# Retention scores masked on three engines, and a weight conversion without its sign step, started at another pace

## The chip, the cores and the metric

The kernel runs on one core of a Trainium2 chip. The metric is the device time of one execution in microseconds (us), and less is better. Five engines work side by side, each through its own instruction stream in order, and wait for one another by semaphores: TensorE does the matrix products, VectorE, ScalarE and GpSimd the element-wise work, and SyncE issues the transfers (DMAs). In the profile they are PE (PEld for its weight loads), DVE, ACT, POOL and SP.

## The reference, cut to what matters

```python
# 4 batches x 8 heads, 576 tokens, head size 64
scores = (1 / sqrt(64)) * q @ k.T
gamma  = 1 - 2.0 ** (-5 - head)
ret    = scores * where(i >= j, gamma ** (i - j), 0)
x  = (ret @ v), heads joined           # 2304 tokens x 512
h  = x @ w_in                          # 512 -> 2048
x2 = (h * clip(h + 3, 0, 6) / 6) @ w_out     # 2048 -> 512
h2 = x2 @ w2_in                        # 512 -> 1024
solu = h2 * softmax(h2)
out  = layernorm(solu) * g_ln @ w2_out # 1024 -> 512
```

All weights arrive as 64-bit floats, read as pairs of 32-bit integers: index 1 is the upper word (sign, 11 bits of exponent, 20 of mantissa), index 0 the lower.

## The kernel before, in words

**Products in two parts.** Each large product takes every operand as a coarse part plus a rest (both float32r) and adds three products of 128 x 128 weights with 512 columns. So each activation and each weight is split: ScalarE copies the value to the coarse part, and GpSimd or VectorE subtracts to get the rest.

**Attention.** It runs over 16 pairs of heads (`pr` 0 to 15). For each pair TensorE makes `s` (scores of four diagonal blocks of 128 keys by 128 queries for two heads, 128 x 1024 in PSUM, one buffer), `u` (states of four chunks), `z` (the last 64 tokens), and for the pair before it `xp` (values from masked scores and from states, one buffer). VectorE turns `s` into `st` with one multiplication by a mask (L334) that holds one constant for each head, and zeros where the key comes later than the query. ScalarE scales the values `v` by a decay for each key (L320), VectorE steps the states (L350) and multiplies the result by a decay for each query from `tab_sb` (L387, `xa`), and ScalarE and GpSimd split that into `xb`, the input of the next layer.

**Weight conversion.** `Weights.split` (from L112) turns a block of 128 x 512 doubles into coarse part and rest. ScalarE scales the upper words as floats into `wz` (L119). VectorE shifts left by 3 (L122), puts the sign back (L123), masks the exponent out (L124), scales the lower word by it (L125) and adds (L128). ScalarE copies the sum to the coarse part (L130), and VectorE, for every third block GpSimd, subtracts for the rest (L132). Raw data are loaded ahead into two `wraw` buffers, each free again after L125 has read it. There are 48 conversions in the run: 12 during attention (six blocks for `w_in`, then six for `w_out`), 20 more for the other `w_in` and `w_out` blocks from about 190 to 350 us, and 16 for the last layer.

**Order.** Attention yields three times for each pair, so a step `s` counts three to a pair. A conversion is issued at steps 5, 6, 8, 9, 11, 12 and so on (two of three, from pair 1) until the 12 are out. From pair 5 on, two pieces of the next layer (`mlp_a`, six matmuls each) go into every step. A scheduler then sets each engine's order from this; it is fixed when the program is built.

Of the kernel before, what the change touches and what calls it, by code (L numbers as in the profile page):

```python
# [9 lines left out]
F32 = mybir.dt.float32  # L10
# [13 lines left out]
NFF2 = DFF2 // 128  # L24
FA = 6
GAMMA = [1.0 - 2.0 ** (-5 - h) for h in range(H)]
N_DEC = 128 * (H // 2) + H + H // 2
NPAIR = NH // 2
NV = 5
BLOCKS = [(0, 512), (512, 512), (1024, 512), (1536, 512), (2048, 256)]  # L30
# [3 lines left out]
C_ORDER = (2, 4, 3, 0, 1)  # L34
NX = 10
STEP_B = 12
W_LOAD = 4
W_FROM = 5
A_FROM = 5
TAIL = 2  # L40
ACT_W = (1,)
# [14 lines left out]


@with_exitstack
def retention_hardswish_solu_kernel(ctx, tc, kt, qt, kn, vt, w1, w2i, w2o, gln, decay, out):


    nc = tc.nc
    ve, se, ge = nc.vector, nc.scalar, nc.gpsimd
# [25 lines left out]
    class Weights:  # L89
# [22 lines left out]
        def split(self, raw, w, scale=None, done=None):  # L112


            z = p0.tile([128, 512], F32, tag="wz", bufs=2, name="wz")
            t = p0.tile([128, 512], I32, tag="wt", bufs=2, name="wt")
            zi, f = z.bitcast(I32), t.bitcast(F32)

            first = se.activation(out=z, in_=raw[:, :, 1].bitcast(F32), func=ACTF.Copy, scale=2.0 ** -112)  # L119
            if self.pin:  # L120
                tc.keep_in_program_order(first)
            ve.tensor_scalar(out=t, in0=zi, scalar1=3, scalar2=None, op0=ALU.logical_shift_left)  # L122
            ve.scalar_tensor_tensor(out=t, in0=zi, scalar=-2 ** 31, in1=t, op0=ALU.bitwise_and, op1=ALU.bitwise_or)  # L123
            ve.tensor_scalar(out=zi, in0=t, scalar1=-2 ** 23, scalar2=None, op0=ALU.bitwise_and)  # L124
            ve.scalar_tensor_tensor(  # L125
                out=z, in0=raw[:, :, 0].bitcast(U32), scalar=2.0 ** -52, in1=z, op0=ALU.mult, op1=ALU.mult
            )
            ve.tensor_tensor(out=f, in0=f, in1=z, op=ALU.add)  # L128
            if scale is None:
                se.activation(out=w[:, 0], in_=f, func=ACTF.Copy)  # L130
                eng = ge if self.at % 3 == 2 else ve
                eng.tensor_tensor(out=w[:, 1], in0=f, in1=f32(w[:, 0]), op=ALU.subtract)  # L132
            else:
                se.activation(out=w[:, 0], in_=f, func=ACTF.Copy, scale=scale)
                ve.scalar_tensor_tensor(
                    out=w[:, 1], in0=f, scalar=scale, in1=f32(w[:, 0]), op0=ALU.mult, op1=ALU.subtract
                )
            if done:
                done()
# [130 lines left out]
    pa = tc.alloc_tile_pool(name="pa", bufs=1)  # L270
    ps_a = tc.alloc_tile_pool(name="ps_a", bufs=1, space=bass.MemoryType.PSUM)

    decay_sb = pa.tile([128, N_DEC], F32, name="decay_sb")
    tab_sb = [pa.tile([128, S], F32, name=f"tab_sb{p}") for p in range(NP)]
    mask = pa.tile([128, NP, 2, 128], F32, name="mask")
    mask4 = pa.tile([128, NP, 64], F32, name="mask4")
    raws, vs, sts, sts4, states, us, xps = {}, {}, {}, {}, {}, {}, {}
    HEADS = [slice(0, 64), slice(64, 128)]
    CHUNKS = [slice(128 * c, min(128 * c + 128, S)) for c in range(NV)]
# [5 lines left out]
    def mm_a(*args, **kw):  # L285
        tc.keep_in_program_order(nc.tensor.matmul(*args, **kw))  # L286

    def load_pair(pr):

        if pr >= NPAIR:  # L290
            return
        early = pr < EARLY
        if early:
            raw = p0.tile([128, 3, S], F32, tag="w", bufs=FA, name=f"raw{pr}")
            rk, rq, rn = raw[:, 0], raw[:, 1], raw[:, 2, :512]
        else:
            rk = pa.tile([128, S], F32, tag="rk", bufs=2, name=f"rk{pr}")
            rq = pa.tile([128, S], F32, tag="rq", bufs=3, name=f"rq{pr}")
            rn = pa.tile([128, 512], F32, tag="rn", bufs=2, name=f"rn{pr}")
        nc.sync.dma_start(out=rk, in_=kt[pr])  # L300
        nc.sync.dma_start(out=rq, in_=qt[pr])
        if pr == 0:
            nc.sync.dma_start(out=decay_sb, in_=decay)
        if early:
            rv = p0.tile([128, 2 * NV, D], F32, tag="g", bufs=FA, name=f"rv{pr}")
        else:
            rv = pa.tile([128, 2 * NV, D], F32, tag="rv", bufs=2, name=f"rv{pr}")
        nc.sync.dma_start(out=rv, in_=vt[pr])
        nc.sync.dma_start(out=rn, in_=kn[pr])
        raws[pr] = rk, rq, rn.rearrange("p (c d) -> p c d", d=128), rv  # L310

    def prep(pr):

        if pr >= NPAIR:
            return
        rv = raws[pr][3]
        v = vs[pr] = pa.tile([128, 2, NV, D], F32, tag="v", bufs=2, name=f"v{pr}")
        for h in range(2):
            head = 128 * NP + 2 * (pr % NP) + h
            se.activation(  # L320
                out=v[:, h].rearrange("p c d -> p (c d)"),
                in_=rv[:, NV * h:NV * h + NV].rearrange("p c d -> p (c d)"),
                func=ACTF.Copy, scale=decay_sb[:, head:head + 1],
            )

    def scores(pr):

        st = sts[pr] = pa.tile([128, 2, 512], F32, tag="st", bufs=2, name=f"st{pr}")
        sp = ps_a.tile([128, 2, 512], F32, tag="s", bufs=1, name=f"s{pr}")
        k, q, _, _ = raws[pr]  # L330
        for c in range(4):
            for h in range(2):
                mm_a(sp[:, h, CHUNKS[c]], k[HEADS[h], CHUNKS[c]], q[HEADS[h], CHUNKS[c]], start=(c == 0), stop=(c == 3))
        ve.tensor_tensor(  # L334
            out=st.rearrange("p h (c q) -> p h c q", q=128), in0=sp.rearrange("p h (c q) -> p h c q", q=128),
            in1=mask[:, pr % NP].unsqueeze(2).to_broadcast([128, 2, 4, 128]), op=ALU.mult,
        )

    def chunk_states(pr):

        rn, v = raws[pr][2], vs[pr]
        up = ps_a.tile([128, 4, 64], F32, tag="u", bufs=1, name=f"u{pr}")
        state = states[pr] = pa.tile([128, 4, 64], F32, tag="state", bufs=2, name=f"state{pr}")
        for c in range(4):
            for h in range(2):
                mm_a(up[HEADS[h], c], rn[:, c, HEADS[h]], v[:, h, c], start=(c == 0), stop=(c == 3))
        at = 128 * NP + H + pr % NP
        se.activation(out=state[:, 0], in_=up[:, 0], func=ACTF.Copy)
        for c in range(1, 4):
# [94 lines left out]
    g_a = lambda ff: (p0, "g", FA)
    mlp_a = chain.from_iterable(mlp(t, list(range(FA)), g_a, evac_partial) for t in range(3))
# [189 lines left out]
    first = {}  # L635
# [19 lines left out]
    t = B_ORDER[-1]  # L655
# [63 lines left out]
```

## Time and profile before

| what | value |
|---|---|
| median of 3 runs | 715.96 us (714.98 to 716.06) |
| the profiled execution, its own time | 715.41 us |
| its span, first to last instruction | 713.7 us |
| TensorE busy | 680.6 us, 95% of the span |
| VectorE, ScalarE, GpSimd busy | 441.9, 307.2, 249.1 us |
| TensorE busy 0 to 90 us, and 90 to 200 us | 67.63 of 90, 110.00 of 110 us |
| TensorE busy 200 to 360, and 360 to 520 us | 152.36 of 160, 160.00 of 160 us |
| mean granted clock of TensorE | 0.978 |

The profiled execution's time is its span and 1.71 us around it. A stretch in which TensorE is busy from end to end is not proof that TensorE is at its best there, but one with gaps shows that something else came last. The attention pairs can be followed by the scores matmuls, which open each pair.

### The profile page before, as it was taken

The numbers are of one execution on the slowest core, as the hardware profiler recorded it, in microseconds if no ns is written. First come the engines' busy times: TensorE is split into PE (matmuls) and PEld (weight loads), VectorE is DVE, ScalarE is ACT, GpSimd is POOL, SyncE is SP. The second block draws the span as 40 slices with busy tenths as digits, with TensorE's granted clock in tenths as the row PEclk, the third lists the DMA queues.
The fourth block names the chain that finished last, engine by engine and source line by source line (L and its number), as shares of the span: only waits on it lengthen the run. The fifth ranks groups of instructions, "written<-read, shape, count | busy, mean of one in ns | idle before, by whom it ended". The sixth has DMA issues, their size and how long they took to land.

```text
span 713.7 us, 10518 instructions
## 1 busy us (share of the span) xinstructions
PE 680.6 (95%) x3968; PEld 560.5 (79%) x3968; DVE 441.9 (62%) x673; ACT 307.2 (43%) x536; POOL 249.1 (35%) x233
## 2 busy tenths in 40 slices
PE   7577899999998999999999999999999999999998
PEld 5565677788886997778778888889988888888887
DVE  3899943240496387925777785411178877776780
ACT  4335442342544435433524524413247555454453
POOL 2233341240533133353633502422236633331333
PEclk8789999999999999999999999999999999999999
DMA  9676666113151533315568365013655643233233
GB/s 332 230 227 206 202 191 197 58 45 74 59 192 45 178 110 100 116 56 181 179 198 272 125 228 180 29 45 130 251 166 133 148 89 74 69 80 74 60 82 81
DMA packets 76259, 97.96 MB, mean 137 GB/s; under 512 B 42672, under 2 KB 44976, under 8 KB 75184
## 3 DMA queue, kind: packets, MB, share of 16 engines
q1 hardware_dynamic: 76208, 97.29, 45.1%
q8 instruction: 31, 0.51, 0.3%
q14 instruction: 20, 0.16, 0.1%
HBM read 63.71 MB, written 24.12 MB: 123 GB/s over the span
## 4 chain that ended last, share of the span: by engine, by line
PE 70%; DVE 12%; DMA 7%; issue 5%; ACT 3%; POOL 1%; SPq 0%; DVEq 0%; POOLq 0%; ACTq 0%
PE h L189 17%; PE x L210 16%; PE o L625 14%; PE h L559 14%; DMA wraw<-in_w_dram 6%; PE acc L210 4%; PE xp L286 3%; DVE wt L122 2%; DVE wt L123 2%; DVE wz L125 2%; ACT wz L119 1%; DVE wt L128 1%; PE s L286 1%; DVE wz L124 1%; PE u L286 1%
## 5 line engine op out<-in xcount | busy, mean ns | idle before, releaser
L204 POOL TENSOR_TENSOR g<-gf,g 128x512 fp32r<-128x512 f32 (+1 forms) x80 | 101.4, 1269 | 218.4 <-ACT g L203 194.7
L210 PE MATMUL x<-g,w 128*128 128x512 f32 x648 | 154.6, 393 | 3.0 <-DVE gf L200 1.5
L210 PEld LDWEIGHTS x<-g,w 128*128 128x128 f32 x648 | 120.0, 188 | 31.1 <-DVE gf L200 2.2
L189 PE MATMUL h<-xb,w 128*128 128x512 f32 (+1 forms) x600 | 137.3, 366 | 3.9 <-ACT w L130 2.4
L189 PEld LDWEIGHTS h<-xb,w 128*128 128x128 f32 x600 | 101.8, 193 | 22.4 <-ACT w L130 2.8
L200 DVE SCALAR_TENSOR_TENSOR gf<-r,h 128x512 f32<-128x512 f32 (+1 forms) x80 | 50.3, 629 | 87.2 <-ACT r L199 70.0
L559 PE MATMUL h<-w2i,x2b 128*128 128x512 f32 x432 | 102.0, 389 | 0.0
L625 PE MATMUL o<-w2o,lt 128*128 128x512 f32 (+1 forms) x456 | 101.0, 378 | 0.0
L625 PEld LDWEIGHTS o<-w2o,lt 128*128 128x128 f32 x456 | 82.5, 188 | 16.0
L559 PEld LDWEIGHTS h<-w2i,x2b 128*128 128x128 f32 x432 | 80.6, 188 | 16.3
L189 PE MATMUL h<-xB,w 128*128 128x512 f32 x360 | 82.4, 389 | 0.0
L180 POOL TENSOR_TENSOR lt<-lT,lt 128x512 fp32r<-128x512 f32 x36 | 46.3, 1305 | 93.8 <-ACT lt L179 93.8
L189 PEld LDWEIGHTS h<-xB,w 128*128 128x128 f32 x360 | 67.6, 188 | 14.0
L203 ACT ACTIVATE g<-gf 128x512 fp32r<-128x512 f32 (+1 forms) x80 | 46.9, 587 | 64.3 <-DVE gf L200 64.2
L199 ACT ACTIVATE r<-h,half 128x512 f32<-128x512 f32 (+1 forms) x80 | 50.7, 636 | 40.1 <-PE h L189 39.8
L210 PE MATMUL acc<-g,w 128*128 128x256 f32 (+1 forms) x312 | 63.8, 328 | 0.7 <-ACT x2p L262 0.5
L122 DVE TENSOR_SCALAR wt<-wz 128x512 int32<-128x512 int32 x48 | 33.4, 695 | 39.4 <-ACT wz L119 39.0
L210 PEld LDWEIGHTS acc<-g,w 128*128 128x128 f32 x312 | 50.5, 191 | 8.3 <-POOL g L204 1.0
L180 POOL TENSOR_TENSOR xb<-xa,xb 128x512 fp32r<-128x512 f32 (+7 forms) x32 | 29.1, 927 | 59.9 <-ACT xb L179 59.9
L128 DVE TENSOR_TENSOR wt<-wt,wz 128x512 f32<-128x512 f32 x48 | 44.8, 934 | 0.6
L119 ACT ACTIVATE wz<-wraw 128x512 f32<-128x512 f32 x48 | 31.5, 662 | 26.7 <-DMA wraw<-in_w_dram 21.4
L130 ACT ACTIVATE w<-wt 128x512 fp32r<-128x512 f32 x32 | 20.2, 631 | 45.0 <-DVE wt L128 45.0
(77 smaller groups left out, 744.1 us busy)
## 6 DMA issues: line engine op xcount, KB each, us to landing
wraw<-in_w_dram SPq DMA_DIRECT2D x32, 512.0 KB, 4.2
rv<-in_vt_dram SPq DMA_DIRECT2D x16, 320.0 KB, 4.7
x2l<-x2s SPq DMA_DIRECT2D x18, 256.0 KB, 5.0
out_dram<-osb SPq DMA_DIRECT2D x17, 256.0 KB, 2.0
x2s<-x2p SPq DMA_DIRECT2D x16, 256.0 KB, 3.7
wraw<-in_w2i_dram SPq DMA_DIRECT2D x8, 512.0 KB, 5.7
w2is<-wsi SPq DMA_DIRECT2D x8, 512.0 KB, 4.2
wraw<-in_w2o_dram SPq DMA_DIRECT2D x8, 512.0 KB, 4.8
```

The costliest lines, as they stand in the source:

```text
L119: first = se.activation(out=z, in_=raw[:, :, 1].bitcast(F32), func=ACTF.Copy, scale=2.0 ** -112)
L122: ve.tensor_scalar(out=t, in0=zi, scalar1=3, scalar2=None, op0=ALU.logical_shift_left)
L128: ve.tensor_tensor(out=f, in0=f, in1=z, op=ALU.add)
L180: ge.tensor_tensor(out=x[:, 1, c], in0=src, in1=f32(x[:, 0, c]), op=ALU.subtract)
L189: nc.tensor.matmul(hp, w1t[ff][:, a, c], xb[t, p][:, b, :n], start=(p == 0 and i == 0), stop=(p == NP - 1 and i == 2),)
L199: se.activation(out=r, in_=hp, func=ACTF.Relu, scale=1.0 / 6.0, bias=half)
L200: ve.scalar_tensor_tensor(out=gf, in0=r, scalar=1.0, in1=hp, op0=ALU.min, op1=ALU.mult)
L203: se.activation(out=g[ff][:, 0], in_=gf, func=ACTF.Copy)
L204: ge.tensor_tensor(out=g[ff][:, 1], in0=gf, in1=f32(g[ff][:, 0]), op=ALU.subtract)
L210: nc.tensor.matmul(acc, w1t[ff][:, a, c], g[:, b], start=(first and i == 0), stop=(last and i == 2))
L559: nc.tensor.matmul(h[:, m], x[:, a, c], w[:, b, m * 512:(m + 1) * 512], start=(d == 0 and j == 0), stop=(d == NP - 1 and j == 2),)
L625: nc.tensor.matmul(op, lt[:, a, ff % 4], w[:, b, c:c + n], start=(ff == 0 and j == 0), stop=(ff == NFF2 - 1 and j == 2),)
```

## The change

**Conversion.** ScalarE's first step becomes Prelu with a slope of 2^32 for negative inputs, which puts the sign where VectorE's shift by 3 leaves it in the sign bit. The sign step (L123) goes. ScalarE makes the coarse part at once from the shifted upper word (`f`), not from the sum, and the sum goes to `z`. So VectorE does four steps and the subtraction where it did five and the subtraction.

**Pace.** The first two loads come at step 2 (before 4). Conversions start at step 4, one for each pair up to pair 4, and two for each pair from then on.

**Scores.** The mask shrinks to head 0 and VectorE multiplies that half alone (128 x 512). ScalarE copies head 1's half out of PSUM with a constant factor, and GpSimd's affine_select then clears the later keys in place. The constant factor is the one that the mask held for that head.

**Tables.** The query decay comes as an input of its own (`place`, 256 KB), loaded behind pair 0's data, and GpSimd copies it to `tab_sb` where ScalarE made 20 copies. The small `decay` table is loaded first of all.

```diff
-W_LOAD = 4
-W_FROM = 5
+W_LOAD = 2
+W_FROM = 4
...
-            first = se.activation(out=z, in_=raw[:, :, 1].bitcast(F32), func=ACTF.Copy, scale=2.0 ** -112)
+            first = se.activation(
+                out=z, in_=raw[:, :, 1].bitcast(F32), func=ACTF.Prelu, scale=2.0 ** -112, alpha=2.0 ** 32
+            )
...
             ve.tensor_scalar(out=t, in0=zi, scalar1=3, scalar2=None, op0=ALU.logical_shift_left)
-            ve.scalar_tensor_tensor(out=t, in0=zi, scalar=-2 ** 31, in1=t, op0=ALU.bitwise_and, op1=ALU.bitwise_or)
+            se.activation(out=w[:, 0], in_=f, func=ACTF.Copy, scale=1.0 if scale is None else scale)
...
-            ve.tensor_tensor(out=f, in0=f, in1=z, op=ALU.add)
+            ve.tensor_tensor(out=z, in0=f, in1=z, op=ALU.add)
...
-                eng.tensor_tensor(out=w[:, 1], in0=f, in1=f32(w[:, 0]), op=ALU.subtract)
+                eng.tensor_tensor(out=w[:, 1], in0=z, in1=f32(w[:, 0]), op=ALU.subtract)
...
         ve.tensor_tensor(
-            out=st.rearrange("p h (c q) -> p h c q", q=128), in0=sp.rearrange("p h (c q) -> p h c q", q=128),
-            in1=mask[:, pr % NP].unsqueeze(2).to_broadcast([128, 2, 4, 128]), op=ALU.mult,
+            out=st[:, 0].rearrange("p (c q) -> p c q", q=128), in0=sp[:, 0].rearrange("p (c q) -> p c q", q=128),
+            in1=mask[:, pr % NP].unsqueeze(1).to_broadcast([128, 4, 128]), op=ALU.mult,
+        )
+        se.activation(out=st[:, 1], in_=sp[:, 1], func=ACTF.Copy, scale=GAMMA[2 * (pr % NP) + 1] ** -128)
+        ge.affine_select(
+            out=st[:, 1], in_=st[:, 1], compare_op=ALU.is_ge, fill=0.0,
+            base=0, pattern=[[0, 4], [1, 128]], channel_multiplier=-1,
         )
...
+        if pr == 0:
+            nc.sync.dma_start(out=place_sb, in_=place)
...
+    nc.sync.dma_start(out=decay_sb, in_=decay)
     for pr in range(EARLY):
...
     for p in range(NP):
-        for c in CHUNKS:
-            se.activation(out=tab_sb[p][:, c], in_=decay_sb[:, 128 * p:128 * p + c.stop - c.start], func=ACTF.Copy)
+        ge.tensor_copy(
+            out=tab_sb[p][:, :512].rearrange("p (c q) -> p c q", q=128),
+            in_=place_sb[:, p].unsqueeze(1).to_broadcast([128, 4, 128]),
+        )
+        ge.tensor_copy(out=tab_sb[p][:, 512:], in_=place_sb[:, p, :64])
...
-        if s >= W_FROM and (s - W_FROM) % 3 != 2:
+        if s >= W_FROM and (s - W_FROM) % 3 < (1 if pr < A_FROM else 2):
             wq.step()
```

What stood on VectorE between pair 3's last-token mask (`st4` of pair 3) and the scores mask of pair 4 (`st4_490`; the number behind the underscore is the buffer's):

```order
L361 TENSOR_TENSOR st43_454<-z3_453,mask4_101 128x64
L122 TENSOR_SCALAR wt_410<-wz_409 128x512
L123 SCALAR_TENSOR_TENSOR wt_410<-wz_409,wt_410 128x512
L124 TENSOR_SCALAR wz_409<-wt_410 128x512
L387 TENSOR_TENSOR xa2_468<-xp2_444,tab_sb2_98 128x576
L125 SCALAR_TENSOR_TENSOR wz_409<-wraw_313,wz_409 128x512
L128 TENSOR_TENSOR wt_410<-wt_410,wz_409 128x512
L122 TENSOR_SCALAR wt_481<-wz_480 128x512
L123 SCALAR_TENSOR_TENSOR wt_481<-wz_480,wt_481 128x512
L132 TENSOR_TENSOR w1_3_179<-wt_410,w1_3_179 128x512
L334 TENSOR_TENSOR st4_490<-s4_491,mask_100 128x1024
L124 TENSOR_SCALAR wz_480<-wt_481 128x512
```

What stands there now, from the scores mask of pair 3 to that of pair 4:

```order
L337 TENSOR_TENSOR st3_374<-s3_375,mask_101 128x512
L358 SCALAR_TENSOR_TENSOR state3_399<-state3_399,decay_sb_95,u3_398 128x64 x2
L126 TENSOR_SCALAR wt_424<-wz_423 128x512
L358 SCALAR_TENSOR_TENSOR state3_399<-state3_399,decay_sb_95,u3_398 128x64
L128 TENSOR_SCALAR wz_423<-wt_424 128x512
L129 SCALAR_TENSOR_TENSOR wz_423<-wraw_254,wz_423 128x512
L369 TENSOR_TENSOR st43_433<-z3_432,mask4_102 128x64
L132 TENSOR_TENSOR wz_423<-wt_424,wz_423 128x512
L395 TENSOR_TENSOR xa2_447<-xp2_412,tab_sb2_99 128x576
L337 TENSOR_TENSOR st4_457<-s4_458,mask_101 128x512
```

One conversion (`wt_424`) now lies between two masks, where the rows before hold the whole of `wt_410` and the start of `wt_481`, and none of the rows is a sign step.

ScalarE before, over the same pairs (`v4` are the scaled values of pair 4, `xb0_2` a split of pair 2's result):

```order
L348 ACTIVATE state3_431<-u3_430 128x64
L130 ACTIVATE w1_2_178<-wt_387 128x512
L119 ACTIVATE wz_409<-wraw_313 128x512
L320 ACTIVATE v4_419<-rv4_333,decay_sb_95 128x320 x2
L179 ACTIVATE xb0_2_470<-xa2_468 128x512
L179 ACTIVATE xb1_2_474<-xa2_468 128x64
L119 ACTIVATE wz_480<-wraw_384 128x512
L130 ACTIVATE w1_3_179<-wt_410 128x512
L348 ACTIVATE state4_525<-u4_524 128x64
L130 ACTIVATE w1_4_180<-wt_481 128x512
```

ScalarE now, from the scaled copy of pair 3's head 1 to that of pair 4:

```order
L341 ACTIVATE st3_374<-s3_375 128x512
L356 ACTIVATE state3_399<-u3_398 128x64
L121 ACTIVATE wz_423<-wraw_254 128x512
L127 ACTIVATE w1_2_164<-wt_424 128x512
L323 ACTIVATE v4_387<-rv4_312,decay_sb_95 128x320 x2
L181 ACTIVATE xb0_2_449<-xa2_447 128x512
L181 ACTIVATE xb1_2_453<-xa2_447 128x64
L341 ACTIVATE st4_457<-s4_458 128x512
```

The scaled copies (`st3`, `st4`) are new and stand behind the splits of the pair before. The coarse part (`w1_2_164`) follows its first step at once.

GpSimd now, from pair 3's clearing of later keys (`st3_374`) on:

```order
L342 AFFINE_SELECT st3_374<-st3_374 128x512
L135 TENSOR_TENSOR w1_2_164<-wz_423,w1_2_164 128x512
L182 TENSOR_TENSOR xb0_2_449<-xa2_447,xb0_2_449 128x512
L182 TENSOR_TENSOR xb1_2_453<-xa2_447,xb1_2_453 128x64
L342 AFFINE_SELECT st4_457<-st4_457 128x512
L182 TENSOR_TENSOR xb0_3_532<-xa3_530,xb0_3_532 128x512
```

Each pair has one AFFINE_SELECT more on GpSimd, in front of the split of the pair before; the TENSOR_TENSOR rows were there before.

## Rows read from the trace of the kernel before

**Rows 1.** TensorE waits, whole span: waiting line, releaser; us in total, times, longest.

```profile
PE u L286 <- ACT v L320: 12.1, 6, 3.9
PE s L286 <- DVE st L334: 4.7, 3, 1.8
PE xp L286 <- DVE xa L387: 4.1, 5, 1.9
PE h L189 <- ACT w L130: 2.4, 1, 2.4
PE x L210 <- DVE gf L200: 1.5, 2, 0.8
...
PE h L189 <- ACT x2p L262: 1.0, 1, 1.0
```

**Rows 2.** Busy time by engine in 20 us stretches: us (count), granted clock, DMA share, GB/s.

```profile
20.00:40.00 20.00, 11.53 (x130) 9.79 (x128) 18.60 (x34) 7.73 (x17) 4.39 (x5) 0.71 0.65 223
...
100.00:120.00 20.00, 20.00 (x219) 15.31 (x218) 7.39 (x16) 5.15 (x12) 2.57 (x3) 1.00 0.66 197
```

**Rows 3.** TensorE in order of time: the scores matmuls of pairs 3, 5, 10, 11.

```profile
22.36 1.16 PE L286 MATMUL s<-rq,rk 64*128 64x128 f32 x16 [1.84 <-DVE st L334]
...
43.75 1.16 PE L286 MATMUL s<-rq,rk 64*128 64x128 f32 x16 [1.39 <-DVE st L334]
...
98.01 1.16 PE L286 MATMUL s<-rq,rk 64*128 64x128 f32 x16
...
106.52 1.16 PE L286 MATMUL s<-rq,rk 64*128 64x128 f32 x16
```

**Rows 4.** VectorE groups, 0 to 100 us: xcount, us busy, mean ns, idle before.

```profile
L334 DVE TENSOR_TENSOR st<-s,mask 128x1024 f32<-128x1024 f32 x11 | 13.4, 1216 | 7.4 <-PE s L286 7.4
L123 DVE SCALAR_TENSOR_TENSOR wt<-wz,wt 128x512 int32<-128x512 int32 x12 | 10.2, 849 | 0.3
L128 DVE TENSOR_TENSOR wt<-wt,wz 128x512 f32<-128x512 f32 x12 | 10.1, 842 | 0.1
L122 DVE TENSOR_SCALAR wt<-wz 128x512 int32<-128x512 int32 x12 | 9.5, 795 | 3.0 <-ACT wz L119 2.6
L125 DVE SCALAR_TENSOR_TENSOR wz<-wraw,wz 128x512 f32<-128x512 uint32 x12 | 9.0, 753 | 0.1
L350 DVE SCALAR_TENSOR_TENSOR state<-state,decay_sb,u 128x64 f32<-128x64 f32 x30 | 8.2, 274 | 0.4
L387 DVE TENSOR_TENSOR xa<-xp,tab_sb 128x576 f32<-128x576 f32 x9 | 6.8, 751 | 2.4 <-PE xp L286 1.4 <-POOL xb L180 1.0
L132 DVE TENSOR_TENSOR w<-wt,w 128x512 fp32r<-128x512 f32 x8 | 6.1, 760 | 1.4 <-ACT w L130 1.3
L124 DVE TENSOR_SCALAR wz<-wt 128x512 int32<-128x512 int32 x12 | 5.0, 417 | 0.1
L200 DVE SCALAR_TENSOR_TENSOR gf<-r,h 128x512 f32<-128x512 f32 x6 | 4.1, 678 | 1.4 <-ACT r L199 1.4
```

**Rows 5.** All engines in order of time, 49 to 52 us: start us, us.

```profile
49.47 2.22 POOL L180 TENSOR_TENSOR xb<-xa,xb 128x512 fp32r<-128x512 f32 x2 [8.06 <-ACT xb L179]
...
49.83 1.68 DVE L128 TENSOR_TENSOR wt<-wt,wz 128x512 f32<-128x512 f32 x1
```

**Rows 6.** ScalarE groups, 0 to 100 us: the first step of the weight conversion.

```profile
L119 ACT ACTIVATE wz<-wraw 128x512 f32<-128x512 f32 x12 | 7.9, 660 | 2.3 <-DMA wraw<-in_w_dram 2.3
```

**Rows 7.** GpSimd groups, 0 to 100 us: the clearing of later keys in the mask.

```profile
L428 POOL TENSOR_SCALAR_AFFINE_SELECT mask<-mask 128x1024 f32<-128x1024 f32 x1 | 1.1, 1092 | 0.0
```

**Rows 8.** DMA queues, 0 to 100 us: packets, MB, share of 16 engines.

```profile
q1 hardware_dynamic: 11344, 23.34, 71.1%
```

**Rows 9.** VectorE and ScalarE in order of time, 301 to 305 us.

```profile
301.66 0.43 DVE L122 TENSOR_SCALAR wt<-wz 128x512 int32<-128x512 int32 x1
...
303.21 0.68 DVE L128 TENSOR_TENSOR wt<-wt,wz 128x512 f32<-128x512 f32 x1
...
303.92 0.63 ACT L130 ACTIVATE w<-wt 128x512 fp32r<-128x512 f32 x1 [1.72 <-DVE wt L128]
```

More of the change, by code (lines that the diff above doesn't have):

```diff
@@ L26 @@
 GAMMA = [1.0 - 2.0 ** (-5 - h) for h in range(H)]
-N_DEC = 128 * (H // 2) + H + H // 2
+N_DEC = H + H // 2
 NPAIR = NH // 2
@@ L58, in retention_hardswish_solu_kernel @@
 @with_exitstack
-def retention_hardswish_solu_kernel(ctx, tc, kt, qt, kn, vt, w1, w2i, w2o, gln, decay, out):
+def retention_hardswish_solu_kernel(ctx, tc, kt, qt, kn, vt, w1, w2i, w2o, gln, decay, place, out):
     nc = tc.nc
@@ L127, in split @@
             )
-            ve.tensor_tensor(out=f, in0=f, in1=z, op=ALU.add)
+            ve.tensor_tensor(out=z, in0=f, in1=z, op=ALU.add)
             if scale is None:
-                se.activation(out=w[:, 0], in_=f, func=ACTF.Copy)
                 eng = ge if self.at % 3 == 2 else ve
-                eng.tensor_tensor(out=w[:, 1], in0=f, in1=f32(w[:, 0]), op=ALU.subtract)
+                eng.tensor_tensor(out=w[:, 1], in0=z, in1=f32(w[:, 0]), op=ALU.subtract)
             else:
-                se.activation(out=w[:, 0], in_=f, func=ACTF.Copy, scale=scale)
                 ve.scalar_tensor_tensor(
-                    out=w[:, 1], in0=f, scalar=scale, in1=f32(w[:, 0]), op0=ALU.mult, op1=ALU.subtract
+                    out=w[:, 1], in0=z, scalar=scale, in1=f32(w[:, 0]), op0=ALU.mult, op1=ALU.subtract
                 )
@@ L273, in retention_hardswish_solu_kernel @@
     decay_sb = pa.tile([128, N_DEC], F32, name="decay_sb")
+    place_sb = pa.tile([128, NP, 128], F32, name="place_sb")
     tab_sb = [pa.tile([128, S], F32, name=f"tab_sb{p}") for p in range(NP)]
-    mask = pa.tile([128, NP, 2, 128], F32, name="mask")
+    mask = pa.tile([128, NP, 128], F32, name="mask")
     mask4 = pa.tile([128, NP, 64], F32, name="mask4")
@@ L301, in load_pair @@
         nc.sync.dma_start(out=rq, in_=qt[pr])
-        if pr == 0:
-            nc.sync.dma_start(out=decay_sb, in_=decay)
         if early:
@@ L318, in prep @@
         for h in range(2):
-            head = 128 * NP + 2 * (pr % NP) + h
+            head = 2 * (pr % NP) + h
             se.activation(
@@ L346, in chunk_states @@
                 mm_a(up[HEADS[h], c], rn[:, c, HEADS[h]], v[:, h, c], start=(c == 0), stop=(c == 3))
-        at = 128 * NP + H + pr % NP
+        at = H + pr % NP
         se.activation(out=state[:, 0], in_=up[:, 0], func=ACTF.Copy)
@@ L424, in retention_hardswish_solu_kernel @@
     for p in range(NP):
+        ge.memset(mask[:, p], GAMMA[2 * p] ** -128)
         for h in range(2):
-            ge.memset(mask[:, p, h], GAMMA[2 * p + h] ** -128)
             ge.memset(mask4[HEADS[h], p], GAMMA[2 * p + h] ** (64 * h - 128))
@@ L429, in retention_hardswish_solu_kernel @@
         out=mask, in_=mask, compare_op=ALU.is_ge, fill=0.0,
-        base=0, pattern=[[0, NP], [0, 2], [1, 128]], channel_multiplier=-1,
+        base=0, pattern=[[0, NP], [1, 128]], channel_multiplier=-1,
     )
@@ L670, in retention_hardswish_solu_kernel @@
     pb.release()
-_INS = ["kt", "qt", "kn", "vt", "w1", "w2i", "w2o", "gln", "decay"]
+_INS = ["kt", "qt", "kn", "vt", "w1", "w2i", "w2o", "gln", "decay", "place"]
 def kernel(**inputs):
@@ L700 @@
     gamma = np.asarray(GAMMA)
-    place = np.arange(128, dtype=np.float64)
-    tab = np.repeat((gamma[:, None] ** (place + 128) / np.sqrt(D)).reshape(NP, 2, 128), 64, axis=1).transpose(1, 0, 2)
-    over = gamma[None, :] ** -place[:, None]
+    b = np.arange(128, dtype=np.float64)
+    tab = np.repeat((gamma[:, None] ** (b + 128) / np.sqrt(D)).reshape(NP, 2, 128), 64, axis=1).transpose(1, 0, 2)
+    over = gamma[None, :] ** -b[:, None]
     step = np.repeat((gamma ** 128).reshape(NP, 2), 64, axis=1).T
-    decay = np.concatenate([tab.reshape(128, NP * 128), over, step], axis=1).astype(np.float32)
-    host = dict(kt=kt, qt=qt, kn=kn, vt=vt, w1=w1, w2i=w2i, w2o=w2o, gln=gln, decay=decay)
+    place = tab.reshape(128, NP, 128).astype(np.float32)
+    decay = np.concatenate([over, step], axis=1).astype(np.float32)
+    host = dict(kt=kt, qt=qt, kn=kn, vt=vt, w1=w1, w2i=w2i, w2o=w2o, gln=gln, decay=decay, place=place)
     nc = _bacc.Bacc("TRN2", target_bir_lowering=False, num_devices=1)
```

## The prediction

> **What bounds the kernel now.** I read the waits of TensorE first, because TensorE is busy 95% of the span, and what is left to win is the time when it isn't, or isn't at full clock. The reader is to see in [rows 1] that its waits are few and sit together. Three of them, for `v` (12.1 us), the masked scores `st` (4.7) and `xa` (4.1), are 20.9 us, and all fall into the first 90 us, the attention pairs with the weight conversion. Three smaller ones (2.4, 1.5, 1.0, together 4.9 us) fall between 200 and 320 us, where the next weights are converted.
>
> Next the busy time by stretch [rows 2]. From 20 to 40 us VectorE works 18.60 of 20 us and TensorE 11.53, at a granted clock of 0.71; ScalarE (7.73) and GpSimd (4.39) are far from full. There VectorE is the bound. From 100 to 120 us it is the other way round: TensorE has no gap, its clock is 1.00, VectorE works 7.39.
>
> Then the scores matmuls, which open the pairs [rows 3]. From pair 3 to pair 5 it is 43.75 - 22.36 = 21.39 us (10.7 a pair), from 5 to 10 it is 98.01 - 43.75 = 54.26 (10.9 a pair), and from 10 to 11 it is 8.51, TensorE's own floor with six pieces of the next layer in a pair. Once pair 10 is reached TensorE is full until about 200 us, so time won before pair 10 stays won, and time won for VectorE behind it is worth nothing until then.
>
> **The change, part by part.** VectorE's means over 0 to 100 us already hold what GpSimd's neighbourhood costs them [rows 4]. A conversion is now 0.795 (L122) + 0.849 (L123) + 0.417 (L124) + 0.753 (L125) + 0.842 (L128) + 0.760 (L132) = 4.42 us. Without L123 it is 3.57.
>
> The mask over 128 x 1024 takes 1.216; half the columns I put at half, 0.61. States (3 x 0.274 = 0.82) and `xa` (0.751) stay. So a pair's attention on VectorE is 0.61 + 0.82 + 0.75 = 2.18 us.
>
> ScalarE's new scaled copy has no row; the nearest is the 0.66 of L119 over as many columns [rows 6], and half the mask, 0.61, bounds it from below. I take 0.66. Prelu has no row either: I take the same 0.66, since the engine's order holds one table load now as before; if it cost twice that, a pair with one conversion would be 0.66 longer. GpSimd's clearing over 128 x 1024 takes 1.092 [rows 7]: half the columns lie between 0.55 and 1.09, and I take 0.6. Nothing reads its result until the next pair, so it is hidden as long as GpSimd isn't late by a pair.
>
> But it sits beside VectorE. In [rows 5] GpSimd starts a split at 49.47 us, and VectorE's L128, 0.68 us elsewhere [rows 9], takes 1.68. Such a hit needs a step of a conversion at that moment; I count half of each clearing, 0.3 us a pair, and keep 0 and 1.09 as ends.
>
> *Pairs 0 to 2.* Counted at nothing. ScalarE loses 20 small copies before the first `v`, but the scaled copy of pair 0 now stands behind the values of pair 1, which wait for their load, and the first conversion moves into pair 1, where ScalarE and VectorE wait for its raw block. The eight copies of the query decay go to GpSimd, which has nothing else before the first split; without that cover they hold up the first clearing, and with it pair 0's `xp`. I keep 3 us to either side.
>
> *Pairs 3 and 4.* One conversion each instead of two. The loop runs through VectorE (3.57 + 2.18 = 5.75 us) and two hand-overs on ScalarE that VectorE waits for, Prelu and the scaled copy in front of it (1.32), and 0.3 for GpSimd: 7.4 a pair. 21.39 - 14.8 = **6.6 us** won. The lower bound of a pair is the 5.75 alone (9.9 won).
>
> *Pairs 5 to 9.* Eight conversions now stand here, three with the subtraction on GpSimd: 8 x 3.57 - 3 x 0.76 = 26.3 us. Five attention pairs are 10.9, six activations (L200, 0.678) 4.1, GpSimd's share 1.5: 42.8 us. TensorE's floor is 5 x 8.51 = 42.6, so both would be full at once. VectorE's fullest was 18.60 of 20, 0.93, and 42.8 / 0.93 = 46.0. 54.26 - 46.0 = **8.3 us** won; at the floor it would be 11.7.
>
> *200 to 320 us.* Shown at one place [rows 9]: TensorE waits 2.4 us for a coarse part. Its L122 starts at 301.66, its sum L128 at 303.21, and the copy L130 at 303.92. Now the copy may start when L122 ends, at 302.09: 1.8 us sooner. The other two waits have ScalarE or VectorE busy with the same chain. Of the 4.9 us I take half, **2.4**; the ends are 0 and 4.9. From 360 to 520 us TensorE has no gap (table above), so the sixteen conversions there win nothing.
>
> Sum: 6.6 + 8.3 + 2.4 = 17.3 us. 713.7 - 17.3 = 696.4 us of span, 698.1 with the 1.7 around it. The profiled execution (715.41) was 0.55 below the median (715.96), so the median should be about **699 us**.
>
> **The rivals.**
>
> *The lock bites fully (705 us).* If every clearing blocked VectorE for the longest 1.09 us, the seven pairs 3 to 9 would lose 7 x (1.09 - 0.3) = 5.5 us more. For it: [rows 5]. Against it: L124's mean of 0.417 us over twelve shows that none of those was hit [rows 4]. [...]
>
> *The transfers bind (708 us).* By 100 us the queue has moved 23.34 MB at 71.1% of the engines' time [rows 8]: 71 us at full share. By pair 10 nearly the same bytes are needed, now at about 83 us (98.01 - 14.9), a share of 0.85. Between 20 and 40 us the share is 0.65 [rows 2], yet there the loads wait for buffers. If it can't pass 0.77 behind waits, pair 10 comes at 92 us, and 6 + 2.4 us are won.
>
> *The late second halves (704 us).* The `w_out` halves are converted in pairs 6 to 9, and their first use is in pair 9. If the last three are late by one conversion and its hand-overs, some 5 us of the 8.3 are gone.
>
> *Both engines mesh (692 us).* Pairs 3 and 4 at 5.75 and pairs 5 to 9 at the floor: 9.9 + 11.7 + 2.4 = 24.0 us.
>
> *Slower (722 us).* PSUM has one scores buffer, so the next pair's scores wait for ScalarE's copy as well as VectorE's mask. In pairs 9 to 15 TensorE has no gap today. If ScalarE, with the splits, `v` and the activations ahead of that copy, kept TensorE waiting 3.3 us a pair there, 7 x 3.3 = 23.1 us would be lost against 17.3. It decides from 2.5 us a pair on. Against it: ScalarE works 5.15 of 20 us at 100 to 120 [rows 2].
>
> *No effect (716 us).* VectorE gets free and another wait of the same length takes its place in pairs 3 to 9. Against it: no other engine is above half in [rows 2].
>
> **How the numbers follow.** Chances: forecast 0.48, meshing 0.14, lock 0.12, transfers 0.12, late halves 0.05, slower 0.05, no effect 0.04. The range from 690.5 to 710 leaves out the last two and tails of the meshing and the transfers, about 0.17. The forecast's own range is 695 to 703. About 0.2% (1.4 us) is what a measurement can tell from no change: faster 0.91, same 0.04, slower 0.05.
>
> **What would show it.** Right: pair 10's scores near 83 us, pairs 3 and 4 near 7.4 us each, TensorE's waits for `v` and `xa` in the first 90 us below 5 us together, pairs 10 to 15 still 8.5 us each, the clearing near 0.6 us, Prelu near 0.66, the 2.4 us wait for the coarse part gone. Wrong: a new wait of TensorE for ScalarE's copy or GpSimd's clearing, `wraw` loads that land later than 5 us, or a pair time above 9.5 us between pairs 5 and 9.

## The result, and the profile after

The changed kernel takes 691.38 us (median of 4 runs, 689.61 to 692.32) beside 716.01 us (the kernel before, with a fourth run): 0.9655 of the time before, 95% interval 0.9633 to 0.9677, 24.6 us less. The profiled execution has a span of 689.5 us. The time lies inside the range, near its lower end, 7.6 us below the forecast of 699 and outside the 695 to 703 us that the forecast itself covered.

The waits of TensorE over the whole span answer to [rows 1]:

```profile
PE xp L289 <- DVE xa L395: 5.7, 5, 2.2
PE u L289 <- ACT v L323: 3.2, 4, 1.9
PE s L289 <- ACT st L341: 2.0, 1, 2.0
PE h L191 <- ACT x2p L264: 1.6, 1, 1.6
...
PE x L212 <- POOL g L206: 1.0, 1, 1.0
PE x L212 <- DVE gf L202: 0.7, 1, 0.7
PE s L289 <- DMA rq<-in_qt_dram: 0.3, 1, 0.3
```

The wait for `v` fell from 12.1 to 3.2 us and the one for `st` from 4.7 to 2.0, now for ScalarE's copy (L341), once, in pair 1. The wait for `xa` grew from 4.1 to 5.7. The waits for a coarse part of the weights and most of those for `gf` are gone. One wait for a transfer appeared, 0.3 us.

The busy times by stretch answer to [rows 2] (TensorE, weight loads, VectorE, ScalarE, GpSimd, then granted clock, DMA share, GB/s):

```profile
20.00:40.00 20.00, 15.09 (x238) 12.62 (x238) 16.07 (x34) 11.31 (x27) 8.45 (x11) 1.00 0.84 280
...
60.00:80.00 20.00, 17.49 (x172) 13.04 (x169) 18.08 (x33) 12.62 (x26) 11.35 (x11) 1.00 0.86 269
...
100.00:120.00 20.00, 20.00 (x179) 15.10 (x179) 4.89 (x12) 6.44 (x12) 3.48 (x4) 1.00 0.48 154
```

From 20 to 40 us the granted clock is 1.00 where it was 0.71, and VectorE works 16.07 us where it worked 18.60. The transfers run at a share of 0.84 and 0.86.

The scores matmuls of pairs 3, 5, 10, 11 and 13 answer to [rows 3]:

```profile
22.43 1.16 PE L289 MATMUL s<-rq,rk 64*128 64x128 f32 x16
...
34.93 1.16 PE L289 MATMUL s<-rq,rk 64*128 64x128 f32 x16
...
86.94 1.16 PE L289 MATMUL s<-rq,rk 64*128 64x128 f32 x16
...
91.44 1.16 PE L289 MATMUL s<-rq,rk 64*128 64x128 f32 x16
...
108.45 1.16 PE L289 MATMUL s<-rq,rk 64*128 64x128 f32 x16
```

and pair 13 before, which [rows 3] doesn't have:

```profile
123.53 1.16 PE L286 MATMUL s<-rq,rk 64*128 64x128 f32 x16
```

Pairs 3 and 4 take 34.93 - 22.43 = 12.50 us (21.39 before). Pairs 5 to 10 take 91.44 - 34.93 = 56.51 us (106.52 - 43.75 = 62.77 before); pair 11 is the mark here because 15 of the 18 matmuls of the next layer that stood behind pair 10's scores now stand before them. From pair 11 to 13 it is 8.5 us a pair in both. So 123.53 - 108.45 = 15.1 us are won by pair 13, and the other 24.2 - 15.1 = 9.1 us of span lie behind attention. Two more marks, before and after, bracket the first part of them:

```profile
172.57 16.48 PE L189 MATMUL h<-xb,w 128*128 128x512 f32 x72
...
241.47 5.68 PE L189 MATMUL h<-xb,w 128*128 128x256 f32 x46
```

```profile
157.50 16.48 PE L191 MATMUL h<-xb,w 128*128 128x512 f32 x72
...
224.88 5.67 PE L191 MATMUL h<-xb,w 128*128 128x256 f32 x46
```

At the first mark the difference is 15.1 us, at the second 16.6. A column of 120 matmuls without a gap (L189, now L191) starts at 376.77 before and at 352.70 after, 24.1 apart. So 7.5 of the 9.1 us fall between about 241 and 377 us of the kernel before.

VectorE's conversion steps up to pair 10 answer to [rows 4], ScalarE's first step and its new copy to [rows 6], GpSimd's clearing (over the whole run, min/median/max in ns) to [rows 7]:

```profile
L132 DVE TENSOR_TENSOR wz<-wt,wz 128x512 f32<-128x512 f32 x11 | 9.9, 911 | 0.1
L126 DVE TENSOR_SCALAR wt<-wz 128x512 int32<-128x512 int32 x11 | 7.6, 701 | 2.7 <-ACT wz L121 2.7
L129 DVE SCALAR_TENSOR_TENSOR wz<-wraw,wz 128x512 f32<-128x512 uint32 x11 | 7.5, 685 | 0.2
...
L128 DVE TENSOR_SCALAR wz<-wt 128x512 int32<-128x512 int32 x11 | 6.4, 592 | 0.1
L337 DVE TENSOR_TENSOR st<-s,mask 128x512 f32<-128x512 f32 x9 | 6.1, 681 | 6.4 <-PE s L289 6.4
```

```profile
L121 ACT ACTIVATE wz<-wraw 128x512 f32<-128x512 f32 x11 | 7.3, 669 | 0.0
...
L341 ACT ACTIVATE st<-s 128x512 f32<-128x512 f32 x9 | 5.3, 587 | 2.8 <-DVE st L337 2.8
```

```profile
L342 POOL TENSOR_SCALAR_AFFINE_SELECT st<-st x16: 630/644/1088, 12.2 to 144.7; 128x512 f32<-128x512 f32 x16
```

The reader sees that the half mask costs 0.68, not 0.61, and that Prelu at 0.67 costs what the copy did. The clearing's median is 0.64, its longest 1.09.

### The profile page after: what moved, and what is told of

Read it like the earlier page. It is cut to its first block, busy times and chain, and to the rows that moved or that the text cites. A ratio compares the mean times of both kernels' runs of the same rounds, so it can differ in the third digit from the quotient of the medians.

```text
span 689.5 us, 10522 instructions
## 1 busy us (share of the span) xinstructions
PE 669.7 (97%) x3968; PEld 554.3 (80%) x3968; DVE 398.7 (58%) x625; ACT 312.0 (45%) x532; POOL 259.2 (38%) x253
## 4 chain that ended last, share of the span: by engine, by line
PE 77%; DVE 7%; DMA 6%; issue 4%; POOL 3%; ACT 2%; SPq 1%; DVEq 0%; POOLq 0%; ACTq 0%
PE h L191 20%; PE x L212 17%; PE o L637 14%; PE h L571 14%; PE acc L212 7%; PE xp L289 2%; DMA xs<-xa 2%; POOL g L206 2%; PE s L289 2%; DVE wz L129 1%; DVE wz L132 1%; DMA wraw<-in_w_dram 1%; DMA rq<-in_qt_dram 1%; DVE wt L126 1%; DVE gf L202 1%
## 5 line engine op out<-in xcount | busy, mean ns | idle before, releaser
L191 PE MATMUL h<-xb,w 128*128 128x512 f32 (+1 forms) x600 | 133.9, 360 | 1.6 <-ACT x2p L264 1.6
L191 PEld LDWEIGHTS h<-xb,w 128*128 128x128 f32 x600 | 99.8, 189 | 18.5 <-ACT x2p L264 2.3
L191 PE MATMUL h<-xB,w 128*128 128x512 f32 x360 | 82.4, 389 | 0.0
L191 PEld LDWEIGHTS h<-xB,w 128*128 128x128 f32 x360 | 67.6, 188 | 14.0
L212 PE MATMUL acc<-g,w 128*128 128x256 f32 (+1 forms) x312 | 62.3, 323 | 0.0
L182 POOL TENSOR_TENSOR xb<-xa,xb 128x512 fp32r<-128x512 f32 (+7 forms) x32 | 26.8, 854 | 35.5 <-ACT xb L181 35.5
L132 DVE TENSOR_TENSOR wz<-wt,wz 128x512 f32<-128x512 f32 x48 | 38.5, 804 | 0.9
L129 DVE SCALAR_TENSOR_TENSOR wz<-wraw,wz 128x512 f32<-128x512 uint32 x48 | 37.0, 773 | 0.8
```

The lines of the kernel that those rows point to most:

```text
L129: ve.scalar_tensor_tensor(out=z, in0=raw[:, :, 0].bitcast(U32), scalar=2.0 ** -52, in1=z, op0=ALU.mult, op1=ALU.mult)
L132: ve.tensor_tensor(out=z, in0=f, in1=z, op=ALU.add)
L182: ge.tensor_tensor(out=x[:, 1, c], in0=src, in1=f32(x[:, 0, c]), op=ALU.subtract)
L191: nc.tensor.matmul(hp, w1t[ff][:, a, c], xb[t, p][:, b, :n], start=(p == 0 and i == 0), stop=(p == NP - 1 and i == 2),)
L212: nc.tensor.matmul(acc, w1t[ff][:, a, c], g[:, b], start=(first and i == 0), stop=(last and i == 2))
```

## The experiments

Every variant is scheduled anew, so the order around an edit can move with it. Each median stands beside that of the kernel before, from the same chip.

**1. Where are the 9 us behind attention from?** Two kernels that have the new conversion on one side only. The first branch holds the new conversion and the second the old one, and `False` marks the weights that are converted in the attention pairs; in the changed kernel with the old conversion late the condition is turned round (`if not self.late`):

```diff
-        def __init__(self, halves, pin):
-            self.pin = pin
+        def __init__(self, halves, pin, late=True):
+            self.pin, self.late = pin, late
...
+            if self.late:
...
+            else:
...
...
-    wq = Weights(w1_halves(range(FA), p0, "w", FA, in_first(FA)), True)
+    wq = Weights(w1_halves(range(FA), p0, "w", FA, in_first(FA)), True, False)
```

The kernel before with the new conversion late:

> The kernel before, with the new conversion for the 36 blocks after attention alone; the 12 in attention, the pace, the scores and the tables are as before. Theory (the early coarse part takes away TensorE's waits between 200 and 360 us, and with them the fall of its clock): about 9 us won, 707 us, no wait of TensorE for the coarse part, no clock of 0.5 behind it. Rival (those 9 us come only because everything there now runs 15 us earlier against the loads): 713 to 716 us.

707.93 us beside 717.3, ratio 0.9861 (0.9841 to 0.9881): 9.4 us won, with pair 13's scores at 123.34, where they were. The changed kernel with the old conversion late:

> The changed kernel, with the old conversion for the 36 blocks after attention. Theory: the 15 us won before pair 11 stay, the 9 us behind it go: 700 us, the scores of pair 11 still near 91.4 us. Rival (earlier arrival is what helped): 692 to 694 us.

701.79 us beside 717.3, ratio 0.9774 (0.9738 to 0.9810), with pair 13's scores at 108.47. The late conversions win their 9 to 10 us with or without the head start. In the kernel with the old ones the wait for a coarse part is back:

```profile
PE h L212 <- ACT w L153: 2.6, 1, 2.6
```

What such a wait costs can be more than its own length. In the kernel before it ends at 304.6 us [rows 9]. These are the stretches behind it, with the granted clock in the third column from the end:

```profile
304.00:306.00 2.00, 1.40 (x4) 1.11 (x5) 1.97 (x4) 0.91 (x2) 0.00 (x0) 0.69 0.00 0
306.00:308.00 2.00, 2.00 (x6) 1.58 (x5) 1.26 (x3) 1.39 (x3) 1.65 (x2) 0.50 0.00 0
308.00:310.00 2.00, 2.00 (x10) 1.61 (x9) 0.18 (x1) 1.67 (x3) 2.00 (x2) 0.96 0.00 0
```

From 306 to 308 us the clock is 0.50, and TensorE starts 6 matmuls where the next stretch at 0.96 starts 10. From 304.6 to 308.6 us it started 11; at 0.227 us each (27.20 us for 120 in the chain) 4 us hold 18, so some 1.6 us were lost on top of 2.4. With the new conversion late, the same part of the program has no such place:

```profile
296.00:302.00 6.00, 6.00 (x29) 4.95 (x28) 4.58 (x7) 3.14 (x6) 3.85 (x3) 1.00 0.00 0
302.00:308.00 6.00, 6.00 (x28) 4.99 (x27) 0.12 (x1) 2.36 (x4) 4.46 (x5) 1.00 0.31 74
```

The fall doesn't follow every such wait. In the changed kernel with the old conversion late, the wait of 2.6 us ends at 290.0 us and the clock behind it stays at 1.00:

```profile
290.00:292.00 2.00, 1.63 (x6) 1.01 (x6) 2.00 (x4) 1.00 (x2) 0.29 (x1) 1.00 0.00 0
```

That execution took 699.94 us all the same, 8.7 more than the profiled one of the changed kernel (691.26). So the waits can cost nearly all of it, and the slow clock is a part that came in one trace and not in the other.

**2. The two edits of the first 90 us, each alone.** The conversion alone is the first three pieces of the diff above without the rest.

> The kernel before with the new conversion everywhere, and nothing else. Theory (VectorE is the bound before pair 9, and a conversion is 0.85 us shorter there): the 9 us behind attention, and 8 to 10 us before it: 697 to 699 us. Rival (the pace is what wins the first 15 us): 706 us.

701.66 us beside 717.3, ratio 0.9789 (0.9765 to 0.9813), pair 13's scores at 118.27. So 5.3 us are won before pair 13, not 8 to 10. VectorE isn't full any more, and yet pairs 3 and 4 take 9.9 and 10.3 us (scores at 21.74, 31.62 and 41.91). In each of them VectorE's shift (L124 there) waits 1.40 us for ScalarE's first step (L119, `wz`), which ScalarE does behind the split of the `xa` that VectorE has only just made. Work and these waits are 19.54 of VectorE's 20 us:

```profile
20.00:40.00 20.00, 11.37 (x134) 9.88 (x136) 16.74 (x31) 8.42 (x20) 5.00 (x5) 0.68 0.74 252
...
28.33 0.92 DVE L124 TENSOR_SCALAR wt<-wz 128x512 int32<-128x512 int32 x1 [1.40 <-ACT wz L119]
```

The pace alone:

```diff
-W_LOAD = 4
-W_FROM = 5
+W_LOAD = 2
+W_FROM = 4
...
-        if s >= W_FROM and (s - W_FROM) % 3 != 2:
+        if s >= W_FROM and (s - W_FROM) % 3 < (1 if pr < A_FROM else 2):
```

> The kernel before with the new pace alone (loads from step 2, conversions from step 4, one a pair up to pair 4). VectorE's sum before pair 10 stays the same. Theory: the twelve old conversions only move, pairs 3 and 4 get shorter and 5 to 9 longer, 712 to 717 us. Rival: the pace wins most of the first 15 us, 703 us.

707.59 us beside 717.3, ratio 0.9870 (0.9843 to 0.9898). The theory missed. Pair 3's, 5's and 13's scores:

```profile
21.27 1.16 PE L286 MATMUL s<-rq,rk 64*128 64x128 f32 x16
...
35.17 1.16 PE L286 MATMUL s<-rq,rk 64*128 64x128 f32 x16
...
113.50 1.16 PE L286 MATMUL s<-rq,rk 64*128 64x128 f32 x16
```

10.0 us are won by pair 13 with the old conversion and the old mask, 8.6 of them by pair 5 (35.17, where it was 43.75). VectorE's sum is the same; what changed is under which pairs it lies. The profiled execution is the slowest of four, 711.31 us beside 707.01 to 707.99: its granted clock is 1.00 from 90 to 200 us, 0.97 from 200 to 300 us and 0.95 from 300 to 380 us. So only the marks up to pair 13 are read here. A new theory was formed on this: pairs 2 to 4 have too little matmul work to hide conversions under, the pairs from 5 on have more.

**3. The change without the pace.**

```diff
-W_LOAD = 2
-W_FROM = 4
+W_LOAD = 4
+W_FROM = 5
...
-        if s >= W_FROM and (s - W_FROM) % 3 < (1 if pr < A_FROM else 2):
+        if s >= W_FROM and (s - W_FROM) % 3 != 2:
```

> The changed kernel with the pace of before (loads from step 4, conversions at two of three steps from step 5). Theory, formed on the run of the pace alone: TensorE has too little of its own in pairs 2 to 4 to hide conversions under, and moving them to pairs with six pieces of the next layer wins 10 us whatever a conversion costs; so 10 us are lost here: 701 us, and pair 13's scores near 118 us where the changed kernel has them at 108.4. Rival (the two parts win the same time, and the shorter conversion alone would do): 694 us.

705.62 us beside 716.5, ratio 0.9842 (0.9815 to 0.9869), pair 13's scores at 122.05. 14 us are lost, more than the 10 expected. The stretch from 20 to 40 us and one wait say why this is worse than the conversion alone:

```profile
20.00:40.00 20.00, 12.85 (x148) 11.11 (x144) 15.99 (x31) 9.57 (x20) 6.46 (x7) 0.60 0.69 226
```

```profile
PE s L289 <- ACT st L341: 5.2, 4, 1.9
```

As with the conversion alone, VectorE is no longer full (15.99 of 20) and yet the pairs take 10 us each; the clock is 0.60, and TensorE waits four times for ScalarE's scaled copy of the scores. Under the old pace the new hand-over is late.

**4. Is the clock part of it?** The same kernel, with TensorE kept at work by 15 matmuls of zeros on 512 columns (bf16) in each of pairs 1 to 4, in three groups of five. A group took 1.25 us (1.86 for the first). Without them the granted clock from 20 to 40 us was 0.60 and the time 705.62 us (experiment 3):

```diff
+    def keep_busy(pr, n):
+        for _ in range(n if 1 <= pr < 5 else 0):
+            mm_a(warm, idle[:, :128], idle[:, 128:], start=True, stop=True)
...
+                keep_busy(pr, 5)
                 chunk_states(pr)
             if pr:
+                keep_busy(pr, 5)
                 values(pr - 1)
...
                 from_states(pr - 1)
+                keep_busy(pr, 5)
```

> [...] Theory (conversions need other work to lie under; the clock matters little, since VectorE and ScalarE set the loop): 703 to 708 us, with the clock near 1.00. Rival (the slow clock in pairs 2 to 5 lengthens the loop, and the pace wins by keeping it up): 696 to 699 us.

701.22 us beside 716.8, ratio 0.9790 (0.9765 to 0.9814), pair 13's scores at 118.40:

```profile
20.00:40.00 20.00, 20.00 (x223) 12.00 (x221) 17.15 (x32) 10.86 (x24) 7.13 (x8) 1.00 0.70 218
```

The clock is 1.00 in place of 0.60, and 4.4 us come back (3.7 by the ratios), although the added matmuls stand in TensorE's way. That lies between the two expectations: of the 14 us that the pace is worth here, some 4 came back with the clock. The edit doesn't set the clock alone, since pair 3's scores start at 28.46 us where they started at 23.77, and the order around them moved. Whether the other 10 us hold more of the clock isn't shown, because the added matmuls have a price of their own, three times 1.25 us a pair.

**5. The pace pushed the other way**, with conversions at every step from step 4 (three a pair):

```diff
-W_LOAD = 4
-W_FROM = 5
+W_LOAD = 2
+W_FROM = 4
...
-        if s >= W_FROM and (s - W_FROM) % 3 != 2:
+        if s >= W_FROM:
```

> The kernel before with conversions pushed forward: one at every step from step 4, three a pair, all twelve before pair 6 (the loads from step 2). Theory (what counts is under how much TensorE work of other kinds the conversions lie): pairs 2 to 5 grow to 3 x 4.4 + 2.8 = 16 us each, and the later pairs run at TensorE's 8.5; pair 13's scores come near 136 us against 123.5, and the time is 724 to 730 us. Rival (the gain of the pace came from the earlier start and loads): 710 to 716 us.

719.5 us beside 716.8, ratio 1.0039 (1.0022 to 1.0056), pair 13's scores at 126.52. Slower, although it starts and loads as early as the pace does. So the earlier start isn't what the pace wins by, unless the third conversion in each pair hides a gain of it. The size was off: pair 13's scores are 3.0 us late, not 12, and the time lies between the two expectations.

**6. The scores.** The split alone in the kernel before (the scores part of the diff, with its mask):

> The kernel before with the scores split over three engines and nothing else. Theory: VectorE is spared 0.55 us a pair, GpSimd's clearing gives some of it back, and ScalarE stands in the way of the next scores: 714 to 717 us. Rival (VectorE's relief counts in full, 0.55 us in each of pairs 2 to 8): 712 us.

718.57 us beside 716.5, ratio 1.0025 (1.0007 to 1.0043): not a gain, a loss at the edge of what can be told. The change without it (L337 to L342 as the old L334, and the mask for both heads):

> The changed kernel with VectorE's one multiplication over both heads, as before. Theory (the split is worth little): 690 to 693 us. Rival (VectorE's relief counts in full): 695 to 696 us.

691.32 us beside 716.5, ratio 0.9651 (0.9627 to 0.9675), against 0.9655 with it: the split is worth nothing that can be measured. And the clearing made twice:

```diff
         ge.affine_select(
             out=st[:, 1], in_=st[:, 1], compare_op=ALU.is_ge, fill=0.0,
             base=0, pattern=[[0, 4], [1, 128]], channel_multiplier=-1,
         )
+        ge.affine_select(
+            out=st[:, 1], in_=st[:, 1], compare_op=ALU.is_ge, fill=0.0,
+            base=0, pattern=[[0, 4], [1, 128]], channel_multiplier=-1,
+        )
```

> The changed kernel with GpSimd's clearing made twice for each pair, 16 instructions of 0.64 us more. Theory (each costs VectorE at most half its length, in the few pairs where VectorE is behind): 692 to 694 us. Rival (each blocks VectorE for its whole length, or for 1.09 us, in pairs 3 to 9): 696 to 699 us.

693.91 us beside 716.5, ratio 0.9681 (0.9655 to 0.9707): 2.5 us by the medians and 1.9 by the ratios for 16 clearings more, with intervals that overlap, so it is not clear of noise. Its trace has a wait for the clearing itself:

```profile
PE xp L289 <- POOL st L346: 1.2, 1, 1.2
```

**7. What is left when only two edits stand, and a more even pace.** The conversion and the pace alone:

> The kernel before with the new conversion and the new pace alone: scores and tables as before. Theory (the scores and the tables are worth nothing together): 690 to 693 us. Rival (the tables win some 2 us at the start): 694 us.

692.22 us beside 716.8, ratio 0.9657 (0.9629 to 0.9684). It can't be told from the whole change, so the scores and the tables together are worth nothing that shows. The even pace, again with VectorE's one multiplication over both heads:

```diff
-        if s >= W_FROM and (s - W_FROM) % 3 < (1 if pr < A_FROM else 2):
+        if s in (4, 7, 10, 13, 15, 17, 19, 21, 23, 25, 26, 28):
```

> The changed kernel with VectorE's one multiplication over both heads, and the conversions spread more evenly after pair 4: steps 4, 7, 10, 13, 15, 17, 19, 21, 23, 25, 26, 28, so that no pair but the last two holds two at once. Theory (in the changed kernel pairs 8 and 9 take 2 to 4 us more than TensorE's floor, because two conversions are interleaved there): 689 us. Rival (the last halves come later and TensorE waits for them): 692 to 694 us.

692.66 us beside 716.8, ratio 0.9672 (0.9647 to 0.9698). No gain beside the same kernel with the pace of the change (0.9651, experiment 6). The rival's wait for a rest of the weights is there, 0.7 us, and a longer one for an activation:

```profile
PE x L212 <- DVE gf L202: 1.6, 1, 1.6
...
PE x L212 <- DVE w L135: 0.7, 1, 0.7
```

## Why the prediction was right in sign, and short in size

**What bounds the kernel before.** The place was right: 15.1 us came from the pairs up to 10. That VectorE is the bound there was half of it. With the old pace and the conversion alone shortened, VectorE works 16.74 of 20 us and the loop still takes 10 us a pair (experiment 2): it runs through VectorE and, behind it, ScalarE's hand-over, 1.4 us in each pair. The prediction had such hand-overs in its sum for pairs 3 and 4. TensorE's slow clock was in the rows ([rows 2], 0.71) and not in the sum.

**Pairs 0 to 2, at nothing.** Right: pair 3's scores start at 22.43 (22.36 before). As feared, ScalarE's copy for pair 0 holds up pair 1, by 2.0 us.

**Pairs 3 and 4, 6.6 us.** Measured 8.9. The pair was counted at 7.4 us and took 6.25.

**Pairs 5 to 9, 8.3 us.** Measured to pair 11, 62.77 - 56.51 = 6.3. The two errors nearly cancel, so that the sum of 14.9 met 15.1 is partly luck. The working shared the gain between the shorter conversion, the half mask and the pace by VectorE's sum. Alone, the conversion wins 5.3 us by pair 13, the pace 10.0, the split scores nothing. They add up: 5.3 + 10.0 = 15.3.

**200 to 320 us, 2.4 us, with 4.9 as the upper end.** This is the step that failed, and most of what the forecast missed: a term that was mis-sized, and an end that was no bound. The mechanism was right, as the coarse part waits for one VectorE step in place of five, but it measured 9.1 us in the changed kernel and 9.4 by itself (experiment 1). The end of 4.9 added up three waits of TensorE alone. Beside those three [rows 1] the kernel before has these waits from 200 to 400 us:

```profile
PE x L210 <- ACT g L203: 1.5, 1, 1.5
...
PE h L189 <- POOL w L132: 0.5, 1, 0.5
PE acc L210 <- ACT x2p L262: 0.5, 1, 0.5
PE acc L210 <- POOL g L204: 0.3, 1, 0.3
```

They are 2.8 us, 7.7 with the other three; in the changed kernel only the waits for `x2p` (1.6) and for GpSimd's `g` (1.0) are left there, 2.6. That is 5.1 us less waiting by the list. Where the other 4 us are can be seen by the same matmuls in both traces, ahead of the wait for the coarse part, behind it, and twelve matmuls later:

```profile
301.38 0.84 PE L210 MATMUL acc<-g,w 128*128 128x512 f32 x3
304.61 1.11 PE L189 MATMUL h<-xb,w 128*128 128x512 f32 x2 [2.38 <-ACT w L130]
...
309.03 0.84 PE L189 MATMUL h<-xb,w 128*128 128x512 f32 x3
```

```profile
282.42 0.84 PE L212 MATMUL acc<-g,w 128*128 128x512 f32 x3
283.10 0.84 PE L191 MATMUL h<-xb,w 128*128 128x512 f32 x3
...
285.82 0.84 PE L191 MATMUL h<-xb,w 128*128 128x512 f32 x3
```

They are 18.96, 21.51 and 23.21 us apart. So this one wait cost 2.55 us and the slow clock behind it 1.70, close to the 1.6 of experiment 1. Of the rest of the 9.1, 1.5 us came between 172 and 241 us, 2.4 by 301 us and 0.9 behind 309 us, where the list has 0.9, 1.3 and 0.5 us less waiting. The list leaves out a little of a wait, as here (2.38 of 2.55). What else makes these stretches shorter isn't settled; it is at most the 2.2 us by which marks and list differ.

**The rivals.** *The lock:* seen again at one place, as VectorE's sum step takes 1.67 us from 61.27 on beside GpSimd:

```profile
60.78 1.61 POOL L206 TENSOR_TENSOR g<-gf,g 128x512 fp32r<-128x512 f32 x1 [1.62 <-ACT g L205]
...
61.27 1.67 DVE L132 TENSOR_TENSOR wz<-wt,wz 128x512 f32<-128x512 f32 x1
```

GpSimd's ends at 62.39 us and VectorE's step 0.55 us behind it; the median of that step up to 360 us is 0.69. On VectorE the steps of a conversion are the ones that get longer: in the kernel before, L128 takes from 0.677 to 1.780 us up to 360 us, while the mask (L334) stays within 1.209 to 1.225 and `xa` (L387) within 0.741 to 0.759 in all 16 pairs. That one engine locks the other out was not shown. But the price over the kernel was small: doubling the clearings cost about 2 us, not clear of noise, and undoing the split, which leaves them out, gained nothing. *The transfers:* the share rose to 0.84 and 0.86 and TensorE waited 0.3 us for one. ScalarE waited 0.5 us in all for raw blocks up to 100 us, less than before (2.3, [rows 6]). They don't bind here. *The late second halves:* at 86 us TensorE waits 0.3 us for a rest of the weights, and at 79 us 0.7 for an activation; spreading the conversions made it no better. *Meshing:* its time came true, 692 us, but not its way, so that the range held the result is in part luck: pairs 5 to 10 stayed above the floor by 56.51 - 51.06 = 5.5 us. *Slower:* in pairs 9 to 15 TensorE has no wait for ScalarE's copy. The mechanism itself exists, as the four waits under the old pace show, 5.2 us together (experiment 3). *No effect:* out.

**What would show it.** Right: the wait for the coarse part is gone, the clearing takes 0.64 and Prelu 0.67 us, and from pair 11 to 13 a pair takes 8.5 us. Not as said: pair 10's scores come at 86.94 us, not near 83, as most of its work on the next layer now stands before them; the waits for `v` and `xa` together are 8.9 us, not below 5; pairs 3 and 4 took 6.25 us each, not 7.4. Three of the signs of being wrong came as well: TensorE's new wait of 2.0 us for ScalarE's copy, raw blocks that land in 5.3 us in the median up to 100 us (4.4 before), and 10.0 us for pair 5 and 10.9 for pair 8 where 9.5 was the limit. Pairs 5 to 9 fell 2 us short of their term; which of these cost it isn't settled.

## What to carry to other kernels

Where a side job runs beside the main one, ask under which stretch it lies before asking how long it is: moving conversions out of the pairs where TensorE worked 11.53 of 20 us [rows 2] won 10.0 us by pair 13, twice what shortening each by a fifth did (5.3). Price a wait of TensorE with what may follow it: a gap of 2.4 us was followed by a stretch at a granted clock of 0.50 that cost 1.7 us more, while one of 2.6 us in another run was not. And hand work to another engine only where the receiving engine's place in the order is early enough: the same split of the scores cost nothing under one pace and was waited for under the other.

## What the runs showed of the hardware

The mean granted clock from 20 to 40 us was 0.71 before, 0.60 in the change without the pace and 1.00 in the changed kernel, so the order of a side job decided the clock that TensorE ran at there. In the kernel before, 1 us stretches show 0.50 from 25 to 31 and from 36 to 41 us, and 1.00 from 32 to 35 us. Filling TensorE's gaps with matmuls of zeros gave 1.00 again and gained 4.4 us (experiment 4). Behind waits of TensorE for the coarse part, 2.4 and 2.6 us long, the clock fell to 0.50 in one trace and stayed at 1.00 in the other (experiment 1). Halving the masked columns in PSUM took VectorE's step from 1.216 to 0.68 us, not to a half.
